# Decode kernel with kept keys: keys of all kept heads read whole, and four changes at start and end

## The chip, the cores and the metric

The kernel runs on one core of a Trainium2 chip. The metric is device time in microseconds (us); lower is better. The core has five engines that run side by side: TensorE (PE, matmuls; PEld is its weight load), VectorE (DVE), ScalarE (ACT), GpSimd (POOL) and SyncE (SP), which here issues every transfer. Transfers are moved by 16 DMA engines. Each engine executes its own instructions in program order, and waits for others by semaphores.

## The reference, cut to what matters

One decode step, 8 sequences, one new token each. Two layers, with the same weights and the same caches in both; a layer is attention over cached keys and values and then a small feed-forward block:

```
x = x + attention(layernorm(x))     # q = x@wq, 32 query heads, 8 key/value heads
x = x + silu(layernorm(x) @ w1) @ w2
# and both lines once more
# attention per sequence b and head g: 4 query rows against 8192 cached keys of 128 numbers:
# p = softmax(q k^T / sqrt(128)); o = p v; then o @ wo
```

k_cache and v_cache have the shape 8 x 8 x 8192 x 128 in bf16, so keys and values of one (b, g) are 2 MB each, 268 MB in all per pass over both. wq and wo have 4 MB each, w1 (512 x 1792) and w2 (1792 x 512) 1.8 MB each.

## The kernel before, in words

The work is a list of 128 **tasks** (layer, b, g), made by `make_tasks`: one task is attention of one sequence over one head in one layer. Each task is cut into four granules k of 2048 positions, and a granule takes two places in a count of **positions** p that runs over the whole program (8 per task, 1024 in all). The loop over p at the end of `_build` writes out by hand what is emitted at each p: transposes of keys one position ahead (`emit_t_until`), scores (`emit_s`), products with values 14 positions behind the scores (`emit_pv`, LP = 14), the softmax of a task in the next task's positions (`soft`), then `emit_own`, `emit_join`, `emit_fold` and `emit_norm`, which bring the result of a task into one column per query head. Since every engine works in order, the place in this loop sets what stands behind what.

SBUF holds an arena of 28 **slots** of 512 KB. Values are loaded in both layers. Of the keys, the heads 3 to 7 (KEEP = 20 granules, five heads) are **kept**: loaded and transposed in layer 0, and left in place until the same sequence's task in layer 1 has scored them. So 20 slots may be bound by kept keys. `plan_loads` orders all loads by the position at which they are due (`need`), and gives each a slot and the position after which it may be issued (`after`). A kept head is given four aligned slots when its first load is placed. `READ[g]` says how many granules one load of keys takes: 1 for heads 0 to 2, 4 for heads 3 to 5, 2 for heads 6 and 7. A load of w granules has rows of w x 4 KB per partition. In layer 0 `emit_s` scores a kept head once per load (so columns w x 128 wide, in 16 products), in layer 1 once per task with 512 columns.

All loads are issued by SP through one queue, in the order of the program: four key loads, wq, the loads that need no free slot, the rest of the weights (`load_rest`: wo, w1, w2), and then `issue_until(p)` at each position. A load into a used slot waits for the engine that used it last; everything behind it on SP waits too. At the start, x is loaded ahead of the first keys (line 412), and used when `ident`, built by POOL, is ready.

At the end the last task's values are multiplied, `emit_own` (ACT) and three `emit_join` operations (DVE) pick the four diagonal blocks out of a 128 x 512 result, `emit_fold` sums the partitions in one fp32 product, `emit_norm` scales, `wo_part` projects, and `last_block` computes the second feed-forward block for all eight sequences: layernorm with mean and variance by products with constants, `gain` by Ln, Exp and one correction step, the normalised `xnT`, the products with w1 in two halves (SCp banks), silu, the products with w2, and the output. The constants lie in the slot that is free earliest (`last_constants`, emitted at position 1016).

A feed-forward chunk of 128 hidden units f is f = 128 o + q: chunk o is a run of w1's columns, and w2's partition q holds 14 rows of 1 KB, one of each chunk.

Of the kernel before, what the change touches and what calls it, by code (L numbers as in the profile page):

```python
# [6 lines left out]
DH = 128  # L7
# [9 lines left out]
GPG = 2  # L17
NSLOT = 28
SCORED = 2
READ = (1, 1, 1, 4, 4, 4, 2, 2)  # L20
KEEP = 20
LT = 1
PRE = 10
LP = 14
EARLY = 4
WO_FROM = 36
NTP = 2
NSCP = 2
# [3 lines left out]
KB = 512  # L32
QUAD = 32
# [2 lines left out]
JOIN_AT = 1  # L36
FOLD_AT = 3
XW = 4
PIECES = (2, 2, 4)
NQS = 4  # L40
NAT = 2
CW = 32
SETTLE = 1
HALVES = 2

BF16 = mybir.dt.bfloat16
FP32 = mybir.dt.float32
INT32 = mybir.dt.int32
ACT = mybir.ActivationFunctionType
# [191 lines left out]
def _build(ctx, nc, A_x, A_k_cache, A_v_cache, A_wq, A_wo, B_w1, B_w2, out):  # L241
# [120 lines left out]
    def op(eng, inst_fn, reads=(), writes=()):  # L362
        reads = [res(n) if isinstance(n, str) else n for n in reads]
        writes = [res(n) if isinstance(n, str) else n for n in writes]
        syn.acquire(eng, reads, writes)
        inst = inst_fn()
        tok = syn.mark(inst, eng)
        syn.release(tok, reads, writes)
        return tok

    def dma(eng, out_ap, in_ap, counter, reads=(), writes=()):
        reads = [res(n) if isinstance(n, str) else n for n in reads]
        writes = [res(n) if isinstance(n, str) else n for n in writes]
        syn.acquire(eng, reads, writes)
        tok = counter.next_tok()
        eng.dma_start(out_ap, in_ap).then_inc(counter.sem, 16)  # L376
        syn.release(tok, reads, writes)
        return tok

    def mm_group(steps, reads=(), writes=()):  # L380
        def run():
            inst = None
            for f in steps:
                inst = f()
            return inst
        return op(pe, run, reads, writes)
# [21 lines left out]
    with nc.Block() as block:  # L408

        @block.sync  # L410
        def _(sync_eng):
            dma(sp, Xr[0:B, :], x_in, wsem["x"], writes=["P"])

            op(pool, lambda: pool.memset(ident[:, :], 1.0), writes=["ident"])
            op(
                pool,
# [40 lines left out]
                dma(sp, wq_sb[:, :, :], A_wq.rearrange("(kt p) n -> p kt n", p=128), wsem["wq"], writes=["wq"])  # L457

            def load_rest():
                dma(sp, wo_sb[:, :, :], A_wo.rearrange("(h p) d -> p h d", p=128), wsem["wo"], writes=["wo"])  # L460
                dma(sp, w1_sb[:, :, :], B_w1.rearrange("(kt p) f -> p kt f", p=128), wsem["w1"], writes=["w1"])
                dma(sp, w2_sb[:, :, :], B_w2.rearrange("(ft p) d -> p ft d", p=128), wsem["w2"], writes=["w2"])

            for _n in range(NGRAN):
                issue(queue.pop(0))
            load_wq()
            issue_until(-2)
# [141 lines left out]
            def emit_pv(i):  # L609
                ti = i // GPT  # L610
                b, g, k, _h = where(i)
                slot = v_slot[(b, g, k)]
                ob, pb = ti % 2, ti % NPT
                steps = [
                    lambda t=t: pe.matmul(  # L615
                        OTp[ob][t * QUAD:t * QUAD + USED, :],
                        PT[pb][:, k, t].rearrange("p x r -> p (x r)"),
                        ARENA[:, slot * SLOT + t * KB:slot * SLOT + (t + 1) * KB],
                        start=(k == 0), stop=(k == NGRAN - 1),
                    )  # L620
                    for t in range(NQ)
                ]
                mm_group(steps, reads=[r_half(slot, 0), r_half(slot, 1), f"PT{pb}"], writes=[f"OT{ob}"])

            def emit_own(ti):
                ob = ti % 2
                op(act, lambda: act.activation(joint, OTp[ob][:, 0:DH], ACT.Copy, scale=own_x[:, 0:1]),  # L627
                   reads=[f"OT{ob}", "own_x"], writes=["P"])

            def emit_join(ti):  # L630
                ob = ti % 2
                for x in range(1, XW):
                    op(dve, lambda x=x: dve.scalar_tensor_tensor(  # L633
                        joint, OTp[ob][:, x * DH:(x + 1) * DH], own_x[:, x:x + 1], joint, op0=ALU.mult, op1=ALU.add),
                       reads=[f"OT{ob}", "own_x", "P"], writes=["P"])

            def emit_fold(ti):
                ob = ti % 2
                mm_group([
                    lambda: pe.matmul(OTp[ob][:, 0:REP], joint, hm[:, :], start=True, stop=True)  # L640
                ], reads=["P", "hm"], writes=[f"OT{ob}"])
# [231 lines left out]
            mean_w = spare[:, 0:128]  # L873
            words = spare[:, 128:].bitcast(FP32)
            var_w, c32, q32 = words[:, 0:128], words[:, 128:128 + KT * B], words[:, 160:160 + KT * B]
            part, gain, step_ = words[:, 192:192 + B], words[:, 200:200 + B], words[:, 208:208 + B]

            def last_constants():
                op(dve, lambda: dve.memset(mean_w, 1.0 / D), writes=r_calm + ["mean_w"])
                op(dve, lambda: dve.memset(var_w, 1.0 / D), reads=r_calm, writes=["var_w"])  # L880

            def last_block():

# [6 lines left out]
                    for k in range(KT)  # L890
# [3 lines left out]
                op(dve, lambda: dve.tensor_tensor(  # L894
                    c3, x1[:, :, :], QSp[:, 0:B].unsqueeze(1).to_broadcast(wide), ALU.subtract),
                   reads=["XT1", "QS"], writes=["c32"])
                op(dve, lambda: dve.tensor_tensor(q32, c32, c32, ALU.mult), reads=["c32"], writes=["q32"])
                op(dve, lambda: dve.tensor_reduce(part, q3.rearrange("p k b -> p b k"), AX.X, ALU.add),
                   reads=["q32"], writes=["part"])
                mm_group([lambda: pe.matmul(QSp[:, B:2 * B], var_w, part, start=True, stop=True)],  # L900
                         reads=["var_w", "part"], writes=["QS"])
                var = QSp[:, B:2 * B]
                op(act, lambda: act.activation(gain, var, ACT.Ln, bias=eps[:, 0:1], scale=GUESS ** -2),
                   reads=["QS", "eps"], writes=["gain"])
# [6 lines left out]
                op(dve, lambda: dve.tensor_tensor(xnT[:, :, :], c3, gain.unsqueeze(1).to_broadcast(wide), ALU.mult),  # L911
                   reads=["c32", "gain"], writes=["xnT"])

                cut = [FT * j // HALVES for j in range(HALVES + 1)]
                for j, (lo, hi) in enumerate(zip(cut, cut[1:])):
                    n = (hi - lo) * B
                    bank, rb = SCp[j % NSCP], f"SC{j % NSCP}"
                    mm_group([
                        lambda o=o, k=k: pe.matmul(bank[:, (o - lo) * B:(o - lo + 1) * B], w1_sb[:, k, o * 128:(o + 1) * 128], xnT[:, k, :],
                                                   start=(k == 0), stop=(k == KT - 1))  # L920
                        for o in range(lo, hi) for k in range(KT)
                    ], reads=["w1", "xnT"], writes=[rb])
                    ev, re = E[:, lo * B:hi * B], f"e_{j}"
                    op(act, lambda: act.activation(ev, bank[:, 0:n], ACT.Exp, scale=-1.0), reads=[rb, "P"], writes=[re])
                    op(dve, lambda: dve.tensor_scalar(ev, ev, 1.0, None, op0=ALU.add), reads=[re], writes=[re])
                    op(dve, lambda: dve.reciprocal(ev, ev), reads=[re], writes=[re])
                    op(dve, lambda: dve.tensor_tensor(hsT[:, lo * B:hi * B], bank[:, 0:n], ev, ALU.mult),
                       reads=[rb, re], writes=[f"hs_{j}"])
# [11 lines left out]
                for j in range(2):  # L940
# [7 lines left out]
                op(act, lambda: act.copy(Xr[0:B, w:D], SCp[1][0:B, 0:w]),  # L948
                   reads=["SC1"] + [f"e_{j}" for j in range(HALVES)], writes=["P2"])

            chain = []
# [4 lines left out]
            ntask = len(tasks)  # L956

            kept_from = min(g for g, _k in kept)

# [5 lines left out]
            for p in range(NG + LP + GPT + FOLD + 1):  # L965
# [32 lines left out]
                if done >= 0 and done % GPT == 0 and done // GPT < ntask:  # L998
                    tj = done // GPT
                    emit_norm(tj)  # L1000
                    layer, b, _g = tasks[tj]
                    if layer == 0:
                        heads[b].append(_g)
                    elif b == B - 1:
                        heads[B].append(_g)
                    if layer == 0 and tj == last0[b]:
                        assert not chain and turn[0] == b
                        chain.extend([lambda b=b: add_heads(b)] * (HKV - summed[b]) + chain_of(b))
                        chain_b[0] = b
# [41 lines left out]
```

## Time and profile before

| what | value |
|---|---|
| median of 3 runs | 1164.85 us (1164.71 to 1164.93) |
| the profiled execution | 1164.56 us |
| its span, first to last instruction | 1162.4 us |
| busy: PE, DVE, ACT, POOL | 730.0, 744.6, 322.9, 116.7 us |
| read from HBM | 465.05 MB, 400 GB/s over the span |
| packets under 2 KB (semaphore writes among them) | 18144 of 116572 |
| values: loads of 512 KB | 512, 11.0 us from issue to landing |
| keys: loads of 512 KB, 1 MB, 2 MB | 192, 32, 24 |
| wo, w1 and w2 landing after issue | 35.0 us; 26.5 us (median of the two) |
| DVE transposes of keys | 352, 1.236 us each |

How to read it: a packet is one contiguous row of a transfer. The page counts busy time of an engine as a share of the span; the row of DMA digits is the mean busy share of the 16 DMA engines in each fortieth of the span (29 us). In a line of a group, the first numbers are busy us and mean ns of one, and behind the second bar stands how long the engine was idle just before these instructions, and which instruction or transfer ended that. In a table by stretches each engine's busy us stands with its instructions, then the granted clock of TensorE, the DMA share (above 1 where packets of one engine overlap) and GB/s. In the chain of waits a line is start, us, and what ran.

### The profile page before, as it was taken

To read this page: it belongs to the slowest core of one execution; us is meant where nothing else is said; L and a number is where in the kernel's file an instruction comes from. 1 tells how busy PE (TensorE), PEld (TensorE's weight loads), DVE (VectorE), ACT (ScalarE), POOL (GpSimd) and SP (SyncE) were. 2 spreads that over 40 slices of the span, in tenths; PEclk is the share of its full clock that TensorE was granted. 3 is DMA by queue.
4 is the path that set the end of the run, shared out by engine and by line. 5 is a ranking of instruction groups with operands and counts; after the bars stand their busy time and mean duration, and the time that the engine had idled before them with its cause. 6 is when DMAs were issued, how large, how long until landed. Compare 5 with 4: busy or idle time off the path is not lost.

```text
span 1162.4 us, 27108 instructions
## 1 busy us (share of the span) xinstructions
PE 730.0 (63%) x11006; PEld 351.6 (30%) x11006; DVE 744.6 (64%) x1782; ACT 322.9 (28%) x759; POOL 116.7 (10%) x296
## 2 busy tenths in 40 slices
PE   1526677656765576567656676667666676657665
PEld 1212342223322342124222342234222332234233
DVE  3827674776557675767467755777477755767473
ACT  0203224223332233222422233222322232223322
POOL 0000101001110011001100011001100011001110
PEclk9995566555765566555855556555755576555655
DMA  9999999999999999999999999999999999999993
GB/s 369 394 397 411 408 408 414 416 410 402 404 418 413 409 402 417 414 409 402 413 414 413 404 394 416 416 409 407 409 417 411 407 403 419 412 408 403 409 408 159
DMA packets 116572, 466.84 MB, mean 402 GB/s; under 512 B 12240, under 2 KB 18144, under 8 KB 108768
## 3 DMA queue, kind: packets, MB, share of 16 engines
q1 hardware_dynamic: 116448, 465.11, 100.0%
q8 instruction: 87, 1.43, 0.5%
q14 instruction: 37, 0.30, 0.1%
HBM read 465.05 MB, written 0.01 MB: 400 GB/s over the span
## 4 chain that ended last, share of the span: by engine, by line
DMA 55%; SPq 15%; PE 12%; DVE 10%; issue 4%; ACT 3%; POOL 1%; DVEq 0%; ACTq 0%
DMA arena<-in_A_v_cache_dram 55%; SPq L376 15%; PE OTp L615 4%; DVE E L633 3%; DVE arena L485 2%; PE SCp L551 2%; PE MISC L737 2%; PE OTp L640 2%; PE TPp L596 1%; ACT E L578 1%; DVE row L562 1%; ACT PT L600 1%; POOL tops L567 1%; ACT E L627 1%; DVE row L574 1%
## 5 line engine op out<-in xcount | busy, mean ns | idle before, releaser
L485 DVE STREAM_TRANSPOSE arena<-arena 128x1024 int32<-128x1024 int32 x352 | 434.3, 1236 | 152.1 <-DMA arena<-in_A_k_cache_dram 151.7
L615 PE MATMUL OTp<-arena,PT 128*16 128x512 bf16 x2048 | 282.0, 553 | 295.7 <-DMA arena<-in_A_v_cache_dram 274.7
L578 ACT ACTIVATE E<-SCp,row 128x512 bf16<-128x512 f32 x128 | 181.9, 1421 | 596.0 <-DVE row L574 585.5
L551 PE MATMUL SCp<-arena,QB 128*16 128x128 bf16 (+2 forms) x4608 | 254.5, 366 | 20.5 <-DVE arena L485 14.0
L633 DVE SCALAR_TENSOR_TENSOR E<-OTp,row,E 128x128 f32<-128x128 f32 x384 | 131.4, 342 | 116.2 <-ACT E L627 105.0
L615 PEld LDWEIGHTS OTp<-arena,PT 128*16 128x16 bf16 x2048 | 50.3, 91 | 435.8 <-DMA arena<-in_A_v_cache_dram 401.1
L551 PEld LDWEIGHTS SCp<-arena,QB 128*16 128x16 bf16 x4608 | 107.3, 110 | 103.9 <-issue 52.5
L567 POOL PARTITION_ALL_REDUCE tops<-top x128 | 47.5, 371 | 582.2 <-DVE top L564 435.6
L596 PE MATMUL TPp<-ident,E 128*128 128x128 bf16 x512 | 71.7, 288 | 33.7 <-ACT E L578 32.6
L587 POOL PARTITION_ALL_REDUCE ssa<-ssm x128 | 55.8, 436 | 359.9 <-ACT ssm L585 359.9
L600 ACT COPY PT<-TPp 128x256 bf16<-128x256 bf16 x128 | 47.6, 372 | 156.1 <-PE TPp L596 156.1
L640 PE MATMUL OTp<-row,E 128*128 128x4 f32 x256 | 70.2, 345 | 24.4 <-DVE E L633 24.4
L562 DVE TENSOR_REDUCE row<-SCp 128x1 f32<-128x512 f32 x128 | 84.5, 660 | 0.7 <-PE SCp L551 0.7
L640 PEld LDWEIGHTS OTp<-row,E 128*128 128x128 f32 x256 | 59.0, 287 | 85.5 <-DVE E L633 49.9
L596 PEld LDWEIGHTS TPp<-ident,E 128*128 128x128 bf16 x512 | 40.8, 124 | 101.9 <-ACT E L578 72.0
L755 PE MATMUL MISC<-at,wo 128*128 128x32 bf16 x1024 | 37.3, 187 | 18.8 <-DVE row L571 12.7
L627 ACT ACTIVATE E<-OTp,row 128x128 f32<-128x128 f32 x128 | 47.5, 371 | 3.7 <-PE OTp L615 3.7
L737 PE MATMUL MISC<-xnT,wq 128*128 128x32 bf16 (+1 forms) x1152 | 35.6, 186 | 14.1 <-DVE xnT L724 14.1
L737 PEld LDWEIGHTS MISC<-xnT,wq 128*128 128x128 bf16 x1152 | 34.6, 105 | 20.6 <-issue 18.4
L755 PEld LDWEIGHTS MISC<-at,wo 128*128 128x128 bf16 x1024 | 32.9, 105 | 25.4 <-DVE at L650 22.3
L585 ACT ACTIVATE ssm<-row 128x4 f32<-128x4 f32 x128 | 37.9, 296 | 3.8
L525 DVE TENSOR_TENSOR QB<-QSp,row 128x64 bf16<-128x64 f32 x128 | 25.8, 202 | 19.6 <-PE QSp L512 19.5
(94 smaller groups left out, 302.6 us busy)
## 6 DMA issues: line engine op xcount, KB each, us to landing
arena<-in_A_v_cache_dram SPq DMA_DIRECT2D x512, 512.0 KB, 11.0
arena<-in_A_k_cache_dram SPq DMA_DIRECT2D x192, 512.0 KB, 8.3
arena<-in_A_k_cache_dram SPq DMA_DIRECT2D x24, 2048.0 KB, 22.3
arena<-in_A_k_cache_dram SPq DMA_DIRECT2D x32, 1024.0 KB, 19.9
wq<-in_A_wq_dram SPq DMA_DIRECT2D x1, 4096.0 KB, 16.5
wo<-in_A_wo_dram SPq DMA_DIRECT2D x1, 4096.0 KB, 35.0
w<-in_B_w_dram SPq DMA_DIRECT2D x2, 1792.0 KB, 26.5
E<-in_A_x_dram SPq DMA_DIRECT2D x1, 8.0 KB
```

Source lines behind the costliest of these rows:

```text
L376: eng.dma_start(out_ap, in_ap).then_inc(counter.sem, 16)
L485: op(dve, lambda: dve.transpose(words, words), reads=[r_half(slot, 0), r_half(slot, 1)], writes=[r_half(slot, 0), r_half(slot, 1)])
L551: lambda n=n, t=t: pe.matmul(SCp[bank][t * QUAD:t * QUAD + USED, lo * 128:(lo + len(slots)) * 128], QB[qn][:, n, :], keys(t, n), start=(n ...
L562: op(dve, lambda: dve.tensor_reduce(rowmax[:, :], SCp[bank][:, :], AX.X, ALU.max), reads=[f"SC{bank}"], writes=["rowmax"])
L578: op(act, lambda: act.activation(P[:, :].rearrange("p (x j k) -> p k x j", x=CPB, k=NGRAN), SCp[bank][:, :].rearrange("p (k x j) -> p k x ...
L596: lambda c=c: pe.transpose(tpv[:, c, :], P[:, c * 128:(c + 1) * 128], ident[:, :])
L600: op(act, lambda: act.copy(PT[pb][:, :, :, :, :].rearrange("p a t x r -> p x t a r"), tpv.rearrange("p x (t q) -> p x t q", q=QUAD)[:, :, ...
L615: lambda t=t: pe.matmul(OTp[ob][t * QUAD:t * QUAD + USED, :], PT[pb][:, k, t].rearrange("p x r -> p (x r)"), ARENA[:, slot * SLOT + t * KB ...
L633: op(dve, lambda x=x: dve.scalar_tensor_tensor(joint, OTp[ob][:, x * DH:(x + 1) * DH], own_x[:, x:x + 1], joint, op0=ALU.mult, op1=ALU.add ...
L640: lambda: pe.matmul(OTp[ob][:, 0:REP], joint, hm[:, :], start=True, stop=True)
L737: lambda o=o, k=k: pe.matmul(MISC[:, o * n:o * n + w], w_sb[:, k, o * 128:(o + 1) * 128], rhs_of(k).to_broadcast([128, w]) if n == 1 else ...
L755: lambda o=o, h=h: pe.matmul(MISC[:, o * w:(o + 1) * w], wo_sb[:, h, o * 128:(o + 1) * 128], rhs_of(h).to_broadcast([128, w]) if n == 1 el ...
```

## The change

READ becomes 4 for heads 6 and 7: their keys come in one load of 2 MB and are scored by 16 products of 512 columns in layer 0 too. Four changes at the ends go with it: (1) x is issued behind the first key load; (2) w1 is loaded ahead of wo, row by row into w2's place, and at position 30 four ACT copies deal its columns out into w1's place, chunk ft taking the columns f = 14 q + ft; then w2 is loaded with partition q holding rows 14 q to 14 q + 13, which is one run of 14 KB; (3) the last task takes two of the four blocks at a time in its products with values (XL = 2), so that two blocks are left; they are copied as they are, and selected and folded by two fp32 products with `own_last`; the joins go; (4) in `last_block` the products with w1 run on the centred, not yet scaled values, two blocks ahead of the variance product and the rest behind it, and `gain` is multiplied onto the results.

```
-READ = (1, 1, 1, 4, 4, 4, 2, 2)
+READ = (1, 1, 1, 4, 4, 4, 4, 4)
...
-            dma(sp, Xr[0:B, :], x_in, wsem["x"], writes=["P"])
...
             def load_rest():
+                dma(sp, undealt, B_w1.rearrange("(kt p) f -> p kt f", p=128), wsem["w1"], writes=["w2"])
                 dma(sp, wo_sb[:, :, :], A_wo.rearrange("(h p) d -> p h d", p=128), wsem["wo"], writes=["wo"])
-                dma(sp, w1_sb[:, :, :], B_w1.rearrange("(kt p) f -> p kt f", p=128), wsem["w1"], writes=["w1"])
-                dma(sp, w2_sb[:, :, :], B_w2.rearrange("(ft p) d -> p ft d", p=128), wsem["w2"], writes=["w2"])
...
+            def deal_w1():
+                for k in range(KT):
+                    op(act, lambda k=k: act.copy(w1_sb[:, k, :].rearrange("p (ft q) -> p ft q", ft=FT),
+                                                 undealt[:, k, :].rearrange("p (q ft) -> p ft q", ft=FT)),
+                       reads=["w2"], writes=["w1"])
+                dma(sp, w2_sb[:, :, :], B_w2.rearrange("(p ft) d -> p ft d", p=128), wsem["w2"], writes=["w2"])
+
+            issue(queue.pop(0))
+            dma(sp, Xr[0:B, :], x_in, wsem["x"], writes=["P"])
+            for _n in range(1, NGRAN):
                 issue(queue.pop(0))
...
+                w = XL if ti == ntask - 1 else XW
                 steps = [
-                    lambda t=t: pe.matmul(
-                        OTp[ob][t * QUAD:t * QUAD + USED, :],
...
+                    lambda t=t, y=y: pe.matmul(
+                        OTp[ob][t * QUAD:t * QUAD + w * REP, 0:w * DH],
...
-                    for t in range(NQ)
+                    for y in range(CPB // w) for t in range(NQ)
...
             def emit_own(ti):
                 ob = ti % 2
+                if ti == ntask - 1:
+                    op(act, lambda: act.copy(E[:, 0:XL * DH], OTp[ob][:, 0:XL * DH]), reads=[f"OT{ob}"], writes=["P"])
+                    return
...
             def emit_join(ti):
                 ob = ti % 2
+                if ti == ntask - 1:
+                    return
...
             def emit_fold(ti):
                 ob = ti % 2
+                if ti == ntask - 1:
+                    mm_group([
+                        lambda x=x: pe.matmul(OTp[ob][:, 0:REP], E[:, x * DH:(x + 1) * DH], own_last[:, x * REP:(x + 1) * REP],
+                                              start=(x == 0), stop=(x == XL - 1))
+                        for x in range(XL)
+                    ], reads=["P", "own_last"], writes=[f"OT{ob}"])
+                    return
...
+                op(act, lambda: act.copy(xnT[:, :, :], c3), reads=["c32"], writes=["xnT"])
...
+                rise(0, AHEAD)
                 mm_group([lambda: pe.matmul(QSp[:, B:2 * B], var_w, part, start=True, stop=True)],
                          reads=["var_w", "part"], writes=["QS"])
+                rise(AHEAD, cut[1])
+                for lo, hi in zip(cut[1:], cut[2:]):
+                    rise(lo, hi)
...
-                op(dve, lambda: dve.tensor_tensor(xnT[:, :, :], c3, gain.unsqueeze(1).to_broadcast(wide), ALU.mult),
-                   reads=["c32", "gain"], writes=["xnT"])
...
+                    op(dve, lambda: dve.tensor_tensor(
+                        scaled[j].rearrange("p (o b) -> p o b", b=B), SCp[j][:, 0:n * B].rearrange("p (o b) -> p o b", b=B),
+                        gain.unsqueeze(1).to_broadcast([128, n, B]), ALU.mult),
+                       reads=[f"SC{j}", "gain"], writes=[f"scaled_{j}"])
...
-                    op(act, lambda: act.activation(ev, bank[:, 0:n], ACT.Exp, scale=-1.0), reads=[rb, "P"], writes=[re])
+                    op(act, lambda: act.activation(ev, scaled[j], ACT.Exp, scale=-1.0), reads=[f"scaled_{j}", "P"], writes=[re])
...
+                if p == DEAL_AT:
+                    deal_w1()
                 issue_until(p)
```

`rise(lo, hi)` is the group of w1 products of the blocks lo to hi into bank SCp[j], four products a block; AHEAD is 2, and the halves are cut at block 7 of 14.

More of the change, by code (lines that the diff above doesn't have):

```diff
@@ L25 @@
 EARLY = 4
+DEAL_AT = 30
 WO_FROM = 36
@@ L38 @@
 XW = 4
+XL = 2
 PIECES = (2, 2, 4)
@@ L44 @@
 HALVES = 2
+AHEAD = 2
 BF16 = mybir.dt.bfloat16
@@ L459, in load_rest @@
             def load_rest():
+                dma(sp, undealt, B_w1.rearrange("(kt p) f -> p kt f", p=128), wsem["w1"], writes=["w2"])
                 dma(sp, wo_sb[:, :, :], A_wo.rearrange("(h p) d -> p h d", p=128), wsem["wo"], writes=["wo"])
-                dma(sp, w1_sb[:, :, :], B_w1.rearrange("(kt p) f -> p kt f", p=128), wsem["w1"], writes=["w1"])
-                dma(sp, w2_sb[:, :, :], B_w2.rearrange("(ft p) d -> p ft d", p=128), wsem["w2"], writes=["w2"])
-            for _n in range(NGRAN):
+            assert KT * F == FT * D
+            undealt = w2_sb[:, :, :].rearrange("p ft d -> p (ft d)").rearrange("p (kt f) -> p kt f", kt=KT)
+            def deal_w1():
[7 more added lines that the diff above has]
+            for _n in range(1, NGRAN):
                 issue(queue.pop(0))
@@ L613, in emit_pv @@
                 ob, pb = ti % 2, ti % NPT
+                w = XL if ti == ntask - 1 else XW
                 steps = [
-                    lambda t=t: pe.matmul(
-                        OTp[ob][t * QUAD:t * QUAD + USED, :],
-                        PT[pb][:, k, t].rearrange("p x r -> p (x r)"),
-                        ARENA[:, slot * SLOT + t * KB:slot * SLOT + (t + 1) * KB],
-                        start=(k == 0), stop=(k == NGRAN - 1),
+                    lambda t=t, y=y: pe.matmul(
+                        OTp[ob][t * QUAD:t * QUAD + w * REP, 0:w * DH],
+                        PT[pb][:, k, t, y * w:(y + 1) * w].rearrange("p x r -> p (x r)"),
+                        ARENA[:, slot * SLOT + t * KB + y * w * DH:slot * SLOT + t * KB + (y + 1) * w * DH],
+                        start=(k == 0 and y == 0), stop=(k == NGRAN - 1 and y == CPB // w - 1),
                     )
-                    for t in range(NQ)
+                    for y in range(CPB // w) for t in range(NQ)
                 ]
@@ L875, in _ @@
             var_w, c32, q32 = words[:, 0:128], words[:, 128:128 + KT * B], words[:, 160:160 + KT * B]
+            own_last = words[:, 376:376 + XL * REP]
             part, gain, step_ = words[:, 192:192 + B], words[:, 200:200 + B], words[:, 208:208 + B]
@@ L880, in last_constants @@
                 op(dve, lambda: dve.memset(var_w, 1.0 / D), reads=r_calm, writes=["var_w"])
+                op(dve, lambda: dve.tensor_tensor(
+                    own_last.rearrange("p (x r) -> p x r", r=REP), own_x[:, 0:XL].unsqueeze(2).to_broadcast([128, XL, REP]),
+                    hm[:, :].unsqueeze(1).to_broadcast([128, XL, REP]), ALU.mult),
+                   reads=["own_x", "hm"] + r_calm, writes=["own_last"])
             def last_block():
@@ L899, in last_block, with rise @@
                    reads=["q32"], writes=["part"])
+                cut = [FT * j // HALVES for j in range(HALVES + 1)]
+                def rise(lo, hi):
+                    j = max(n for n in range(HALVES) if cut[n] <= lo)
+                    mm_group([
+                        lambda o=o, k=k: pe.matmul(SCp[j][:, (o - cut[j]) * B:(o - cut[j] + 1) * B],
+                                                   w1_sb[:, k, o * 128:(o + 1) * 128], xnT[:, k, :],
+                                                   start=(k == 0), stop=(k == KT - 1))
+                        for o in range(lo, hi) for k in range(KT)
+                    ], reads=["w1", "xnT"], writes=[f"SC{j}"])
+                assert HALVES <= NSCP
+                rise(0, AHEAD)
                 mm_group([lambda: pe.matmul(QSp[:, B:2 * B], var_w, part, start=True, stop=True)],
                          reads=["var_w", "part"], writes=["QS"])
+                rise(AHEAD, cut[1])
+                for lo, hi in zip(cut[1:], cut[2:]):
+                    rise(lo, hi)
                 var = QSp[:, B:2 * B]
@@ L910, in last_block @@
                    reads=["step_", "gain"], writes=["gain"])
-                op(dve, lambda: dve.tensor_tensor(xnT[:, :, :], c3, gain.unsqueeze(1).to_broadcast(wide), ALU.mult),
-                   reads=["c32", "gain"], writes=["xnT"])
-                cut = [FT * j // HALVES for j in range(HALVES + 1)]
+                scaled = [words[:, 256 + lo * B:256 + hi * B] for lo, hi in zip(cut, cut[1:])]
                 for j, (lo, hi) in enumerate(zip(cut, cut[1:])):
[L916 to L922, printed above, removed]
+                    n = hi - lo
+                    op(dve, lambda: dve.tensor_tensor(
+                        scaled[j].rearrange("p (o b) -> p o b", b=B), SCp[j][:, 0:n * B].rearrange("p (o b) -> p o b", b=B),
+                        gain.unsqueeze(1).to_broadcast([128, n, B]), ALU.mult),
+                       reads=[f"SC{j}", "gain"], writes=[f"scaled_{j}"])
                     ev, re = E[:, lo * B:hi * B], f"e_{j}"
-                    op(act, lambda: act.activation(ev, bank[:, 0:n], ACT.Exp, scale=-1.0), reads=[rb, "P"], writes=[re])
+                    op(act, lambda: act.activation(ev, scaled[j], ACT.Exp, scale=-1.0), reads=[f"scaled_{j}", "P"], writes=[re])
+                for j, (lo, hi) in enumerate(zip(cut, cut[1:])):
+                    ev, re = E[:, lo * B:hi * B], f"e_{j}"
                     op(dve, lambda: dve.tensor_scalar(ev, ev, 1.0, None, op0=ALU.add), reads=[re], writes=[re])
                     op(dve, lambda: dve.reciprocal(ev, ev), reads=[re], writes=[re])
-                    op(dve, lambda: dve.tensor_tensor(hsT[:, lo * B:hi * B], bank[:, 0:n], ev, ALU.mult),
-                       reads=[rb, re], writes=[f"hs_{j}"])
+                    op(dve, lambda: dve.tensor_tensor(hsT[:, lo * B:hi * B], scaled[j], ev, ALU.mult),
+                       reads=[f"scaled_{j}", re], writes=[f"hs_{j}"])
                 for j, (lo, hi) in enumerate(zip(cut, cut[1:])):
@@ L949, in last_block @@
                    reads=["SC1"] + [f"e_{j}" for j in range(HALVES)], writes=["P2"])
+            ntask = len(tasks)
             chain = []
@@ L955, in _ @@
             first1 = {b: min(task_at[(1, b, g)] for g in range(HKV)) * GPT for b in range(B)}
-            ntask = len(tasks)
             kept_from = min(g for g, _k in kept)
```

## The prediction

> **What bounds the kernel now.** The page comes first, its row of DMA slices before the list of engines.
>
> ```profile
> DMA  9999999999999999999999999999999999999993
> GB/s 369 394 397 411 408 408 414 416 410 402 404 418 413 409 402 417 414 409 402 413 414 413 404 394 416 416 409 407 409 417 411 407 403 419 412 408 403 409 408 159
> q1 hardware_dynamic: 116448, 465.11, 100.0%
> ```
>
> The DMA engines are full in 39 of the 40 slices; PE is busy 63% and DVE 64%. All 465 MB pass through one queue. So outside the first microseconds and the last sixteen, time goes only if the bytes take less time. The groups by form confirm it: the product with the values waits 274.7 us for its values to land, and 1.9 us for its probabilities.
>
> ```profile
> L615 PE MATMUL OTp<-arena,PT 128*16 128x512 bf16 x2048 | 282.0, 553 | 295.7 <-DMA arena<-in_A_v_cache_dram 274.7 <-issue 16.0 <-ACT PT L600 1.9
> ```
>
> Second view: stretches chosen so that each holds one or two row lengths, and the packets counted in two of them (last column GB/s).
>
> ```profile
> core 0: us, PE busy (x) PEld busy (x) DVE busy (x) ACT busy (x) POOL busy (x), PEclk, DMA share, GB/s
> 51.00:60.00 9.00, 0.64 (x8) 0.00 (x0) 4.06 (x8) 0.00 (x0) 0.37 (x1) 1.00 1.10 348
> 183.00:189.00 6.00, 3.18 (x46) 1.39 (x42) 2.46 (x10) 2.68 (x8) 0.80 (x2) 0.99 1.03 408
> 224.00:242.00 18.00, 10.94 (x112) 3.91 (x112) 14.25 (x29) 4.70 (x10) 1.60 (x4) 0.59 1.02 415
> 449.00:479.00 30.00, 18.79 (x182) 6.65 (x170) 16.65 (x39) 9.36 (x20) 2.83 (x7) 0.56 1.02 418
> ```
> ```profile
> DMA packets 1530, 7.47 MB, mean 415 GB/s; under 512 B 168, under 2 KB 168, under 8 KB 1070
> ```
> ```profile
> DMA packets 2138, 12.53 MB, mean 418 GB/s; under 512 B 238, under 2 KB 238, under 8 KB 1752
> ```
>
> Four row lengths: 1 KB rows (wo, w2) at 348 GB/s; 4 KB rows at 408; 8 KB rows mixed with 4 KB (heads 6 and 7) at 415; 16 KB mixed with 4 KB (heads 3 to 5) at 418. DMA share is above 1 in every one, so the queue is never dry.
>
> **Keys of heads 6 and 7.** Unmixing 224 to 242 us: 1070-168 = 902 packets of 4 KB are 3.69 MB, 9.06 us at 408; the other 3.78 MB take 8.94 us, 423 GB/s. From 449 to 479: 1514 packets, 6.20 MB, 15.20 us; the other 6.33 MB take 14.80 us, 428 GB/s. The two heads are 16 x 2.10 = 33.6 MB: 79.4 us at 423, 78.4 us at 428. Gain 1.0 us; with 410 instead of 408 for the 4 KB rows it is 1.2. I take 1.1, and 0 to 2 as ends, since it is a difference of two fits.
>
> What else these loads move: plan_loads already reserves four aligned slots at the first half, so slots and release positions stay; the second half (K of head 6, half two: after position 25, due at 51) merges into the first (after 23, due 47) and so passes two value loads in SP's queue. These come 1.05 MB, 2.6 us, later in the queue, and the following ones as much earlier. At the plan's leanest positions (tasks 8 to 13, no kept keys loaded) seven loads, 3.67 MB or 9 us, are issued but not yet due, and there nothing changes; so 2.6 us is covered. Cost 0.
>
> Scores of these 16 tasks: 32 products of 256 columns (32.7 us for 512, 0.064 us each) become 16 of 512 (108.4 us for 1024, 0.106 each): PE loses 5.6 us of work that is beside the DMA. But all 1.7 us now follow the last transpose, where 1.0 us did: the softmax starts 0.7 us later. Cover: PV runs 14 positions behind the scores, and the 1.9 us above is all that 512 PV groups ever waited for probabilities. Without that cover it would be 16 x 0.7 = 11 us. Cost 0.
>
> **w2 in 14 KB rows, the deal of w1.** w2 is 1.835 MB: 5.27 us at the 348 of 1 KB rows, 4.30 us at 427 (a row between 8 and 16 KB). Gain 0.95 us (ends 0.75 and 1.0, at the 408 of 4 KB rows and the 428 of 16 KB rows). w1 keeps its rows of 3.5 KB. It goes ahead of wo, so wo lands some 4.6 us later (1.835 MB at the 401 GB/s of 61 to 64 us); its first reader ran at 77.0 us in the trace.
>
> The price is four ACT copies of 128x1792, read at a stride of 28 bytes. No row has that form. Least: the 128x256 copy, 0.372 us (L600), by length 2.6 us each at most; most: the 128x512 exponential with a strided write, 1.42 us (L578), by length 5.0 us each. I take 4 us each, 16 us, near the strided row. They stand in ACT's order where ACT was idle:
>
> ```profile
> 49.75 0.37 ACT L627 ACTIVATE E<-OTp,row 128x128 f32<-128x128 f32 x1
> 76.86 1.42 ACT L578 ACTIVATE E<-SCp,row 128x512 bf16<-128x512 f32 x1 [26.74 <-DVE row L574]
> ```
>
> w1 now lands around 53 us (the 1 KB rows of wo started near 48). The value load that ends this pause follows wo directly, 5.3 us earlier than now, so ACT is wanted at 71.6. 54+16 = 70: covered; at 5.0 us a copy it is 2 us late. SP waits there too, for the deal, before it issues w2, and the loads after position 30 stand behind it. But those issued before it, 14 value and key loads of 10 MB, last 25 us, until about 91 us. Cost 0; it begins to cost when a copy takes over 9 us.
>
> The Trainium skill (SBUF — State Buffer, Door 1: The DMA port swizzle) says that accesses that go to a new 16-byte line each time pay a penalty, which speaks against this read. No row here shows it for ACT; by it the copies lie nearer to 5 us, still inside the cover.
>
> **The start.** The x load stands ahead of the first keys on SP: issued at 0.79 us, the keys at 1.24. Swapped, the stream starts 0.45 us sooner. x is wanted at 9.5 us, when POOL's ident is ready, so it can wait. Gain 0.45 (ends 0 and 0.45).
>
> **The end.** The chain of waits after the last values:
>
> ```profile
> 1148.63 0.38 ACT E L627
> 1149.10 0.36 DVE E L633
> 1149.49 0.36 DVE E L633
> 1149.87 0.36 DVE E L633
> 1150.28 0.60 PE OTp L640 x2
> ...
> 1154.94 0.20 DVE xnT L911
> 1155.19 0.92 PE SCp L919 x28
> 1156.14 0.23 ACT E L924
> ```
>
> Last task: three joins go, 1149.10 to 1150.28 or 1.18 us. The fold becomes two fp32 products: one weight pair more, 0.50 us by the row of L640. The copy is 256 wide instead of 128 (0.36 to 0.5 by L948 and L578): value equal. Its PV has twice as many products of half the columns, 0 to 0.2 us. Gain 0.65 (0.3 to 0.8).
>
> Last block: first-layer products no longer wait for gain. c32 is ready at 1152.57; ACT's copy (0.19, nearest 128x32 row) ends near 1152.8; two blocks run until 1153.1, when the variance product starts as now (1153.10). The other 48 products at 1.66/56 = 0.030 us end near 1155.1, beside Ln, Exp and three DVE steps, which end at 1154.91 as now. Then a 0.22 us scaling, and Exp starts near 1155.25 instead of 1156.14; the second scaling delays no more than the first reciprocal's start. Gain 0.9 (0.6 to 1.1).
>
> **Sum.** 1.1 + 0.95 + 0.45 + 0.65 + 0.9 = 4.05 us. The profiled execution took 1164.56 (span 1162.4 and 2.16 around it): 1160.5. From the median, 1164.85: 1160.8. I say **1160.7**.
>
> **Rivals.** (a) Row length buys nothing and only start and end count: 2.0 us, 1162.8. For it: rates also vary with what the engines do (394 GB/s in two slices of the page). Against: 348, 408, 423, 428 in order of length. The Trainium skill (DMA: Bandwidth & Descriptors, Specifications) counts 512 bytes and up as full rate; by that rule this rival wins, since all rows here are longer. The 348 against 408 speaks against it. Chance 0.09.
> (b) Slower: whole reads starve the values. Each of the 16 loads puts 2.6 us ahead of two value loads; if SP had nothing else out, the queue would run dry each time for the time from issue to first bytes, 1.1 us (keys issued at 1.24, bytes from about 2.3): 17.6 us, less the other 2.95: 1179.5. It cancels all gains from 0.26 us per head. Against: the DMA share of 1.03 from 449 to 479 us, beside heads 3 to 5, which are read so already. Chance 0.07.
> (c) The deal doesn't fit: at 15 us a copy ACT is done at 114, the queue dry from 91: 23 us less 4.05, 1183.8. Over 9 us a copy is twice the dearest row. Chance 0.03.
> (d) The end gains little, since PE and ACT swap one wait for another: 2.5 us in all, 1162.4. Chance 0.06, half of it within 0.2%.
>
> About 0.2%, 2.3 us, can be told from no change. Forecast 0.75: faster. Faster 0.78, same 0.12, slower 0.10. Range: the upper ends, 5.35 us off the profiled execution, give 1159.2; the lower ends, 1.65 us off the median, 1163.2; (a) and (d) lie inside.
>
> **What would show it.** Packets under 2 KB fall by 1792; K issues become 192 and 40 of 2 MB; the stretch of heads 6 and 7 moves at 418 rather than 415 GB/s; last values land about 2.5 us earlier; from there to the end 1.5 us less. Wrong: a DMA slice under 9 between 55 and 110 us (c) or at heads 6 and 7 (b); Exp of the last block not following gain directly.

## The result, and the profile after

The changed kernel takes 1160.77 us (median of 7 runs, 1159.96 to 1162.44), the kernel before 1164.71 beside it: a ratio of 0.9968, 95% interval 0.9958 to 0.9978. The forecast was 1160.7. The profiled execution is the fastest of the seven, 1159.96 us with a span of 1157.8. Single times of the changed kernel lie up to 2.5 us apart, and the interval reaches about 1.1 us to each side. Below, each kernel is set against the kernel before that ran beside it ("3 under" is 3 us less than that one), and a difference of two such numbers is uncertain by some 1.5 us.

The page of the changed kernel, DMA slices and packet counts:

```profile
DMA  9999999999999999999999999999999999999994
GB/s 372 403 400 415 408 408 414 417 411 404 407 419 415 402 407 417 419 401 409 408 416 411 409 401 416 417 407 403 406 419 410 409 401 419 414 408 403 409 408 184
DMA packets 112602, 466.80 MB, mean 403 GB/s; under 512 B 11984, under 2 KB 16096, under 8 KB 106720
```

No slice is under 9 before the last, so neither the deal nor the whole reads leave the queue dry for long; a slice is 29 us, and a gap of a microsecond would not show in it. Packets under 2 KB fall by 2048: the 1792 rows of w2, and 16 semaphore writes for each of the 16 loads that are gone. The second slice, where the weights come, goes from 394 to 403 GB/s.

Stretches of the changed kernel (last column GB/s): 4 KB rows; heads 5 and 6 of sequence 1; heads 6 and 7 of sequence 1, which ran at 415 before (224 to 242 us); heads 3 to 6 of sequence 3. Which keys move when follows from the order of the issues and the sizes of the packets.

```profile
core 0: us, PE busy (x) PEld busy (x) DVE busy (x) ACT busy (x) POOL busy (x), PEclk, DMA share, GB/s
183.00:189.00 6.00, 4.85 (x42) 1.65 (x38) 2.57 (x11) 2.38 (x5) 0.80 (x2) 0.60 1.03 409
210.00:229.00 19.00, 10.58 (x76) 3.25 (x76) 13.24 (x28) 4.70 (x10) 1.60 (x4) 0.59 1.02 419
220.00:239.00 19.00, 11.01 (x92) 3.76 (x92) 13.75 (x28) 4.74 (x10) 1.60 (x4) 0.55 1.02 419
449.00:479.00 30.00, 17.27 (x166) 6.24 (x166) 18.32 (x42) 7.57 (x17) 2.40 (x6) 0.56 1.02 418
```

Heads 6 and 7 move as fast as heads 3 to 5 do. Counted from the packets of the two traces, from the first row of heads 6 and 7 to their last, they moved at 413 GB/s before and move at 416 now, on average over sequences 1 to 7. ACT in order of time, at the deal:

```profile
50.34 0.37 ACT L643 ACTIVATE E<-OTp,row 128x128 f32<-128x128 f32 x1
54.80 13.61 ACT L469 COPY w<-w 128x1792 bf16<-128x1792 bf16 x4 [4.09 <-DMA w<-in_B_w_dram]
71.09 1.42 ACT L590 ACTIVATE E<-SCp,row 128x512 bf16<-128x512 f32 x1 [2.68 <-DVE row L586]
```

The deal starts when w1 has landed, takes 13.6 us, and ends 2.7 us before ACT is wanted. The chain of waits at the end, from the last task's copy to the Exp of the last block:

```profile
1145.79 0.38 ACT E L641
1146.21 1.03 PE OTp L659 x4
1147.26 0.17 DVE QT L675
...
1148.12 0.20 DVE XT L915
...
1148.96 0.23 ACT xnT L927
1149.23 0.38 PE SCp L937 x8
1149.61 0.43 PE QSp L945 x2
1150.04 1.29 PE SCp L937 x48
1151.37 0.23 DVE arena L962
1151.62 0.26 ACT E L967
```

The three joins are gone from it. The 48 products of w1 stand in this chain, but the first scaling did not wait for all of them: it needs blocks 0 to 6, which PE's semaphore reports at 1150.58, and `gain`, which DVE's reports at 1151.28.

The last products with values and the residual (XT), in the kernel before:

```profile
1147.55 1.03 PE L615 MATMUL OTp<-arena,PT 128*16 128x512 bf16 x8
```
```profile
1151.76 0.20 DVE XT L885
```

and these products in the changed kernel:

```profile
1144.71 1.02 PE L628 MATMUL OTp<-arena,PT 128*8 128x256 bf16 x16
```

They begin 2.84 us earlier; the last row of values had ended at 1146.88 and now ends at 1144.02. From the start of these products to the end of the span (1162.4 and 1157.8 us) it was 14.85 us and is 13.09, 1.76 less.

### The profile page after: what moved, and what is told of

The parts are those of the page before. It is cut to its first block, busy times and chain, and to the rows that moved or that the text cites. A ratio compares the mean times of both kernels' runs of the same rounds, so it can differ in the third digit from the quotient of the medians.

```text
span 1157.8 us, 26616 instructions
## 1 busy us (share of the span) xinstructions
PE 725.2 (63%) x10768; PEld 346.7 (30%) x10768; DVE 740.8 (64%) x1781; ACT 336.6 (29%) x764; POOL 116.7 (10%) x296
## 4 chain that ended last, share of the span: by engine, by line
DMA 53%; DVE 15%; PE 13%; SPq 9%; issue 6%; ACT 3%; POOL 1%; DVEq 0%; ACTq 0%; POOLq 0%
DMA arena<-in_A_v_cache_dram 36%; DMA arena<-in_A_k_cache_dram 17%; SPq L379 9%; DVE arena L497 6%; DVE E L651 4%; PE OTp L628 4%; PE SCp L563 3%; DVE row L574 2%; PE TPp L608 2%; PE OTp L665 1%; PE MISC L762 1%; ACT E L590 1%; PE MISC L780 1%; ACT PT L612 1%; DVE top L576 1%
## 5 line engine op out<-in xcount | busy, mean ns | idle before, releaser
L628 PE MATMUL OTp<-arena,PT 128*16 128x512 bf16 (+1 forms) x2064 | 278.5, 550 | 292.3 <-DMA arena<-in_A_v_cache_dram 271.3
L563 PE MATMUL SCp<-arena,QB 128*16 128x128 bf16 (+1 forms) x4352 | 251.1, 375 | 22.6 <-DVE arena L497 16.3
L628 PEld LDWEIGHTS OTp<-arena,PT 128*16 128x16 bf16 (+1 forms) x2064 | 51.2, 92 | 422.0 <-DMA arena<-in_A_v_cache_dram 382.6
L563 PEld LDWEIGHTS SCp<-arena,QB 128*16 128x16 bf16 x4352 | 100.8, 110 | 112.2 <-issue 59.2
```

The source lines that it names most:

```text
L563: lambda n=n, t=t: pe.matmul(SCp[bank][t * QUAD:t * QUAD + USED, lo * 128:(lo + len(slots)) * 128], QB[qn][:, n, :], keys(t, n), start=(n ...
L628: lambda t=t, y=y: pe.matmul(OTp[ob][t * QUAD:t * QUAD + w * REP, 0:w * DH], PT[pb][:, k, t, y * w:(y + 1) * w].rearrange("p x r -> p (x r)"),
```

## The experiments

The theory on record: the queue is always full, so a change in its work counts fully, by the length of the rows; the end counts by its own chain; everything else is covered. The rivals: (a) row length buys nothing, (b) whole reads starve the values, (c) the deal doesn't fit, (d) the end only swaps waits.

### One part at a time

**The whole reads alone**, on the kernel before:

```
-READ = (1, 1, 1, 4, 4, 4, 2, 2)
+READ = (1, 1, 1, 4, 4, 4, 4, 4)
```

> The kernel before with READ 4 for heads 6 and 7 and nothing else. Theory (longer rows move faster, 423 against 428 GB/s on 33.6 MB): 1.1 us under the kernel before, 1163.6, and the stretch of heads 6 and 7 at 418 GB/s instead of 415. Rival (row length buys nothing): 1164.7. Rival (whole reads starve the values): above 1164.7, DMA share under 1 at heads 6 and 7. If the wider spread of the changed kernel's times (1159.96 to 1162.44) comes with the whole reads, it shows here.

Measured: 1163.52 us against 1164.87 (ratio 0.9990, 0.9981 to 0.9999): 1.35 less, and by the interval 0.1 to 2.2. The eleven times spread over 1.4 us, as those of the kernel before do beside them (1164.39 to 1165.83), so the whole reads alone do not bring a wider spread.

**The ends alone**: the changed kernel with the old READ.

> The changed kernel with READ 2 for heads 6 and 7 as before: the four changes at the ends alone. Theory: 1.1 us above the changed kernel, 1161.9. Rival (row length of the keys buys nothing, the ends are all): 1160.8. If the spread comes with the whole reads, this one is as narrow as the kernel before (0.5 us).

Measured: 1161.96 against 1164.87 (0.9976, 0.9968 to 0.9985). It is 2.91 under the kernel before where the changed kernel is 3.94 under its own: 1.0 us for the whole reads, which is within the uncertainty of such a difference.

**The weight loads of before**: in `load_rest` wo, w1, w2 in their old order and rows, no `deal_w1`.

> The changed kernel with the weight loads of before: wo, w1, w2 in 1 KB rows, no ACT copies. Theory: 0.95 us above the changed kernel, 1161.7, and 1792 more packets under 2 KB. Rival (the deal costs as much as the rows save, by holding SP or ACT): 1160.8 or less.

Measured: 1161.76 against 1164.87 (0.9975, 0.9964 to 0.9986), 3.11 under: by the medians the re-laid w2 is worth 0.8 us, also within the uncertainty. The rival (the deal costs as much as the rows save) is not ruled out by these times.

**The end of before**: last task and last block as they were.

> The changed kernel with the last task and the last block of before. Theory: 1.55 us (by the terms of the prediction) to 1.8 us (by the two chains) above the changed kernel: 1162.3 to 1162.6. Rival (the end only swaps one wait for another): 1160.8 to 1161.1.

Measured: 1162.83 against 1164.87 (0.9985, 0.9976 to 0.9993), 2.04 under: the new end is worth 1.9 us, a little more than the uncertainty, and the two traces above have 1.76 for the same. Rival (d) falls.

**x ahead of the first keys again**:

```
-            issue(queue.pop(0))
             dma(sp, Xr[0:B, :], x_in, wsem["x"], writes=["P"])
+            issue(queue.pop(0))
```

> The changed kernel with x issued ahead of the first keys again. Theory (the stream ends as much later as it starts later): 0.45 us above the changed kernel, 1161.2, and the first key load issued at 1.24 us instead of 0.79. Rival (the start is made good before the first wait): 1160.8. The spread of the runs is about 1.4 us, so the trace's issue times and the median of many runs have to be read together.

Measured: 1160.49 against 1164.98 (0.9964, 0.9951 to 0.9978), 4.49 under: not slower than the changed kernel. The start is worth nothing that can be seen. The first 10 us of the two kernels, changed and x first:

```profile
0.00:5.00 5.00, 0.00 (x0) 0.00 (x0) 0.00 (x0) 1.28 (x1) 0.39 (x5) 1.00 0.60 185
5.00:10.00 5.00, 0.00 (x0) 0.00 (x0) 0.00 (x0) 0.00 (x0) 0.12 (x1) 1.00 1.01 400
```
```profile
0.00:5.00 5.00, 0.00 (x0) 0.00 (x0) 0.00 (x0) 1.28 (x1) 0.40 (x5) 1.00 0.53 157
5.00:10.00 5.00, 0.24 (x4) 0.18 (x4) 0.50 (x3) 0.00 (x0) 0.28 (x1) 1.00 1.03 392
```

The keys do go first: 0.93 MB have moved by 5 us instead of 0.79, a lead of 0.35 us. But only the first key load comes earlier; the second is issued at 1.67 us with keys first and at 1.66 with x first, in both behind x and one load. And the lead is lost in the next 5 us. In the eleven kept traces of kernels with keys first, the rate from 5 to 10 us was 328 to 419 GB/s, in seven of them under 360; in the three with x first it was 388, 392 and 414. By 10 us the kernels with keys first had moved 2.73 MB on average, those with x first 2.79. Whether the swap itself slows these microseconds, and by what, is open.

### Is it the rows?

**The same order, two loads**: heads 6 and 7 issued at the place of the whole read, scored in 512 columns, but as two loads with 8 KB rows.

```
+        if d.kind == "K" and d.wide == NGRAN and d.g >= 6:
+            two = cache[d.b, d.g].rearrange("(p k c) d -> k p (c d)", k=2, p=128)
+            for n in range(2):
...
+                dma(sp, ARENA[:, s * SLOT:(s + 2) * SLOT], two[n], slsem[s],
...
```

> The changed kernel, with the keys of heads 6 and 7 issued at the same place in SP's order and scored in 512 columns, but as two loads of 1 MB with 8 KB rows, one right behind the other. Only row length (and 16 more issues) differs from the changed kernel. Theory (the gain of the whole reads is the row length): 1.1 to 1.3 us above it, 1162.0, as with READ 2. Rival (the gain comes from the earlier issue of the second half, or from the wider scores): 1160.8.

Measured: 1161.93 against 1164.98 (0.9974, 0.9964 to 0.9984), 3.05 under: 0.9 us of the gain is gone, as with READ 2. This is as the theory has it, but 0.9 us is within the uncertainty. The stretch of heads 6 and 7 of sequence 1 tells more:

```profile
221.00:240.00 19.00, 11.41 (x92) 3.75 (x92) 15.15 (x32) 4.71 (x10) 1.60 (x4) 0.53 1.02 414
```

It moves at 414 GB/s, as before the change (415), and not at 419. On average over sequences 1 to 7, from the first row of these heads to the last, it is 414 here, 413 with the ends alone, and 416 and 417 in the changed kernel and with the whole reads alone. Against the ends alone, which have the same rows, this kernel has the earlier issue of the second half and the wider scores: 3.05 under against 2.91, so the two together neither cost nor save anything that can be seen. To bring the difference in time out of the uncertainty, all five kept heads were changed.

**All five kept heads in 8 KB rows, and in 4 KB rows**:

```
+READ = (1, 1, 1, 2, 2, 2, 2, 2)
```
```
+READ = (1, 1, 1, 1, 1, 1, 1, 1)
```

> The same with READ 2, rows of 8 KB for all five kept heads. Theory (423 against 428 GB/s on 83.9 MB): 2.3 us above the changed kernel, 1163.1. Rival: 1160.8. A straight line between 4 KB and 16 KB rows would put it at about 1167; a fixed cost per row puts it at a third of the way, since the rows per byte go 4, 2, 1.

> The changed kernel with READ 1 for all five kept heads: their 83.9 MB of keys in rows of 4 KB, the end of the scale opposite to the change. Theory (rate by row length, 408 against 428 GB/s): 9.6 us above the changed kernel, 1170.4; the stretches of kept keys fall from 418 to 408 GB/s. Rival (the rate hangs on what the engines do at the time, not on the rows): within 2 us of 1160.8.

Measured: 1164.07 against 1164.78 with READ 2 (0.9995, 0.9986 to 1.0004), and 1172.17 with READ 1 (1.0064, 1.0051 to 1.0078). Against the changed kernel that is 3.2 and 11.3 us more. Two stretches of kept heads, READ 2 and then READ 1:

```profile
210.00:229.00 19.00, 10.31 (x102) 3.90 (x106) 13.16 (x28) 4.34 (x10) 1.60 (x4) 0.50 1.02 413
467.00:487.00 20.00, 10.58 (x108) 4.04 (x108) 13.59 (x29) 4.69 (x10) 1.61 (x4) 0.55 1.02 415
```
```profile
210.00:229.00 19.00, 8.49 (x140) 4.21 (x132) 12.57 (x26) 4.04 (x8) 1.60 (x4) 0.54 1.03 409
467.00:487.00 20.00, 9.61 (x172) 4.98 (x168) 14.07 (x29) 4.68 (x10) 1.62 (x5) 0.60 1.03 407
```

409, 413 and 419 GB/s with rows of 4, 8 and 16 KB in the same stretch, at DMA shares above 1 in all three. Rival (a) falls: the interval of READ 2 does not touch that of the changed kernel (0.9986 to 1.0004, 0.9958 to 0.9978), and READ 1 lies far above both. The 83.9 MB have 20480, 10240 and 5120 rows; per DMA engine a step takes away 640 and 320. 8.1/640 and 3.2/320 us are 12.7 and 10.1 ns per row, uncertain by some 3 and 5 ns: about a fixed time per row. A straight line in row length would have put 3.8 of the 11.3 us into the first step, not 8.1.

Each step also halves the number of loads, so a fixed time per load would give the same pattern. The packets in the trace of the kernel before tell the two apart. Their median times are 51, 160, 314 and 615 ns for rows of 1, 4, 8 and 16 KB, and 9 ns for the semaphore write that each engine makes per load. The rows of 4 and 16 KB give 38 ns per KB and 8 ns per row. By these medians READ 1 and the changed kernel are 9.1 us apart, of which the semaphore writes are 1.1; by the means, in which a few slow packets count, it is 12.9 us. Measured are 11.3. And wo, a single load, moved at 348 GB/s in rows of 1 KB: 47 ns per row on each engine, against 161 for 4 KB at 408, which makes 9 ns per row where only one load is concerned. So it is the rows, and their fixed time is known to about 8 to 13 ns.

### How far the cover of the deal reaches

Each dealing copy made twice, and four times:

```
-                for k in range(KT):
+                for k in [k for k in range(KT) for _n in range(4)]:
```

> Each of the four dealing copies is made twice. ACT is then held from 54.8 to about 82 us, 11 us past the point where it is wanted (71.1 us). Theory (the cover of the deal is the transfers already issued, about 10 MB or until 91 us, not ACT's pause): no cost, 1160.8, within 0.3. Rival (what covers it is ACT's idle time alone): up to 11 us, 1171.

> Each dealing copy four times: ACT held until about 109 us, SP waiting for it, the queue dry from about 91. Theory: 18 us for the dry queue and 0 to 3 for the slots that are freed late afterwards: 1179 to 1182, and DMA slices under 9 between 90 and 115 us. Rival (the stall is made good later, or never reaches the queue): under 1165.

Measured: twice, 1160.99 against 1164.78 (0.9965, 0.9953 to 0.9978), no cost, though the copies ran from 56.1 to 83.4 us and ACT's next work came 12 us late. Four times, 1182.24 (1.0154, 1.0138 to 1.0169), 21.4 us over the changed kernel, 0.2 us above the theory's range (1179 to 1182). SP's waits and stretches of that kernel:

```profile
SPq L105 <- ACT w L469: 35.6, 1, 35.6
```
```profile
85.00:90.00 5.00, 0.00 (x0) 0.00 (x0) 0.00 (x0) 4.94 (x3) 0.00 (x0) 1.00 0.98 394
90.00:95.00 5.00, 0.00 (x0) 0.00 (x0) 0.00 (x0) 4.97 (x2) 0.00 (x0) 1.00 0.16 64
95.00:100.00 5.00, 0.00 (x0) 0.00 (x0) 0.00 (x0) 4.94 (x3) 0.00 (x0) 1.00 0.00 0
...
110.00:115.00 5.00, 3.53 (x44) 1.59 (x44) 1.76 (x5) 2.35 (x6) 0.43 (x1) 1.00 0.78 267
```

SP waits 35.6 us for one ACT result; PE and DVE stand still long before; but the price is only the time from 91 us, when what was issued has moved, until the transfers are back after 111. What covers a stall is the depth of the queue, not idle time of the engine that stalls.

**The deal without its stride**: the copies read and write in a row. w1's columns then lie in the wrong order.

```
-                    op(act, lambda k=k: act.copy(w1_sb[:, k, :].rearrange("p (ft q) -> p ft q", ft=FT),
-                                                 undealt[:, k, :].rearrange("p (q ft) -> p ft q", ft=FT)),
+                    op(act, lambda k=k: act.copy(w1_sb[:, k, :],
+                                                 undealt[:, k, :]),
```

> The dealing copies read and write their 1792 columns in a row, so w1's columns land in the wrong order and the feed-forward outputs are not the reference's. One look, for the duration of one copy. If the stride of 28 bytes costs nothing, 3.38 us as in the changed kernel; if it has its price, near 1.4 to 2.6 us, by the contiguous 128x256 and 8x256 copies (0.36 us each).

The group by form, changed kernel and then this one:

```profile
L469 ACT COPY w<-w 128x1792 bf16<-128x1792 bf16 x4 | 13.5, 3378 | 4.2 <-DMA w<-in_B_w_dram 4.1
```
```profile
L469 ACT COPY w<-w 128x1792 bf16<-128x1792 bf16 x4 | 6.7, 1684 | 7.1 <-DMA w<-in_B_w_dram 7.0
```

3378 against 1684 ns: the stride doubles the copy. The Trainium skill (SBUF — State Buffer, Door 1: The DMA port swizzle) says that each access to a new 16-byte line pays a penalty; this pair agrees with it, and gives the size here, 1.9 ns an element instead of 0.94. No other stride was run, so it is not shown that the 16-byte line is the cause.

### Going further

If rows are what counts, the keys of heads 0 to 2 can be read in pairs of granules.

```
-            elif (g, k) not in kept:
-                loads.append(Load("K", b, g, k, -1 if i0 < PRE else i0 - LT, i * GPT + (k + 1) * GPG - 1))
+            elif (g, k) not in kept and k % PAIR == 0:
+                loads.append(Load("K", b, g, k, -1 if i0 < PRE else i0 - LT, i * GPT + (k + PAIR) * GPG - 1, PAIR))
...
```

> A version that goes on from the changed kernel: the keys of heads 0 to 2, which are not kept and are read in both layers, come two granules at a time into two adjacent slots, in rows of 8 KB instead of 4 (96 loads of 1 MB for 192 of 512 KB). Rows per DMA engine fall by 12288/16 = 768. Theory (a fixed cost of 10 to 13 ns per row, from READ 1, 2 and 4: 12.7 ns between 4 and 8 KB): 768 x 12.7 = 9.7 us less, 1151.0. Rival (fewer loads under way at the leanest positions, 2.6 MB instead of 3.7 by the plan, so that the queue runs dry at times): the gain is lost in part or whole, 1155 to 1165, with DMA slices under 9 or a DMA share under 1 in the stretches without kept keys, such as 120 to 190 us.

Measured: 1164.62 us against 1164.76 (0.9987, 0.9968 to 1.0007), 3.8 over the changed kernel, twelve times between 1156.17 and 1168.87; the trace is of one at 1167.84. The time is the one that the rival on record has, 1155 to 1165, but its sign does not come: no DMA slice before the last is under 9, and the stretches without kept keys keep a share of 1.00 and more. The two stretches with the largest loss, both with few or no kept keys, this kernel and the changed one:

```profile
380.00:420.00 40.00, 24.34 (x496) 14.43 (x496) 27.21 (x62) 11.45 (x33) 4.78 (x12) 0.54 1.01 387
520.00:580.00 60.00, 37.84 (x744) 21.74 (x744) 37.12 (x100) 18.54 (x49) 7.45 (x19) 0.70 1.00 391
```
```profile
380.00:420.00 40.00, 27.45 (x551) 16.01 (x551) 28.81 (x67) 11.55 (x33) 4.41 (x11) 0.50 1.02 404
520.00:580.00 60.00, 43.13 (x744) 22.55 (x748) 36.47 (x103) 20.17 (x54) 7.62 (x19) 0.64 1.03 410
```

12288 rows fewer, and yet 387 to 391 GB/s instead of 404 to 410, at a slightly lower DMA share. Not every such stretch loses: from 260 to 300 us it is 408 against 405.

By the plan 2.6 MB instead of 3.7 are issued and not yet due at the leanest positions. A count of the two traces, bytes of the transfers issued less bytes of the packets moved, has from 380 to 420 us 2.0 MB on average and at least 1.30 in the changed kernel, and 1.6 MB and at least 0.44 here. The rows themselves took longer: 5% of the 8 KB rows of this kernel took over 1.3 times their median of 309 ns, some over 2 us, where with READ 2 for the kept heads it was 0.3%. A packet that takes long counts as a busy engine, so the share stays at 1. It is not shown that the thin queue is what slows these rows: the loads also lie in other slots here, and no run separates the two. This is the kind of danger that the prediction named for the whole reads; it comes at the heads that take their slots from the common ones, and not at the kept heads, whose four slots were bound anyway.

## Why the prediction was right

| term | forecast, us | measured |
|---|---|---|
| whole reads of heads 6 and 7 | 1.1 | 1.35 alone, 1.0 undone, 0.9 as two halves |
| w2 in long rows | 0.95 | 0.8, within the uncertainty |
| start | 0.45 | 0 (with x first again 0.55 us less, within the uncertainty) |
| end: last task | 0.65 | 0.80 in the trace |
| end: last block | 0.9 | 0.88 in the trace |
| end, together | 1.55 | 1.9 with the end of before, 1.76 in the trace |
| sum | 4.05 | 3.94 |

The first reading carried it: with the queue full in every slice, time in the queue and time in the last chain are the only ones that count, and the parts add up within the uncertainty: 1.35 us for the reads alone and 2.91 for the ends alone, against 3.94. That the median comes within 0.1 us of the forecast is luck: it is itself uncertain by 1.1, and the start, too high by 0.45, is in part made up by the end, too low by 0.2 to 0.35.

The step that failed is "the start". It took the first issue for the start of the stream. The first bytes did come earlier, but the second load did not, and from 5 to 10 us most of the kernels with keys first moved fewer bytes than those with x first, so that nothing of the 0.35 us is left by 10 us.

One reading proved weaker than it looked. A DMA share above 1 was taken to say that the queue is never dry; the paired reads have 1.00 and 1.01 in stretches that lose 17 and 19 GB/s, so the share alone does not say how full the queue is.

Two terms were right with other sizes inside. A dealing copy took 3.4 us, not 4. The fold's two products took 1.03 us (1.10 was reckoned), and its copy of 256 columns 0.37 us, as long as that of 128. In the last block every step came as worked out: the variance product behind two blocks, the 48 other products beside Ln, Exp and three DVE steps, and the Exp 3.50 us after the residual instead of 4.38. The two arms that meet there are not equally long: the products that the first scaling needs were done at 1150.58, 0.70 us before `gain` (1151.28). So a next step would have to shorten the arm of Ln, Exp and three DVE steps, not the products.

That the passed values and the wider scores cost nothing was reckoned from 9 us issued ahead against 2.6 us, and from PV's 14 positions. The run with two halves has both without the longer rows, and lies 0.14 us from the ends alone. This agrees, to within 1.5 us; no run took one of the two without the other.

## What to carry to other kernels

Where the DMA row of the page is full throughout, count rows, not only bytes: here a row cost about 8 to 13 ns of an engine beyond its bytes, from 4 up to 16 KB. Longer rows need larger loads. In this kernel these paid where the space for them was bound already; where it was taken from what is issued ahead, the gain was lost and the times spread over 13 us. And the cover of a stall is read from the queue: bytes issued and not yet moved, divided by the rate.

## What the runs showed of the hardware

A row has a fixed time beyond its bytes: 12.7 ns from 4 to 8 KB and 10.1 from 8 to 16 KB by the times of the runs, with the semaphore writes of the loads in it, and 8 ns by the median packets of 4 and 16 KB. The Trainium skill (DMA: Bandwidth & Descriptors, Why small descriptors are slow) names three cycles a packet and 32 bytes of descriptor as the cost; at the fabric's 850 MHz and 32 bytes a cycle (the same page, Specifications) that is an estimate of some 5 ns. The runs show more, about twice that. Its line of 512 bytes for full rate (Specifications) does not hold here: 348 GB/s with 1 KB rows, and 407 to 409 with 4 KB.

ACT reading bf16 at a stride of 28 bytes took twice the time of a read in a row, 3378 against 1684 ns for 1792 columns.
